# Two token blocks take turns while the first weights are decoded, with PSUM sums of their own

## The chip, the cores and the metric

The kernel runs on one core of one Trainium2 chip. The metric is the device time of one execution in microseconds (us); before the change the median of three runs is 1047.18 us. Five engines work in parallel, each through its own queue in order: TensorE (PE; its weight loads are PEld), VectorE (DVE), ScalarE (ACT), GpSimd (POOL) and SyncE (SP), which here only issues transfers. They wait for one another through semaphores.

## What is computed

A linear attention with a decaying state, then two feed-forward layers (cut from the reference):

```python
for t in range(S):                      # batch 4, 8 heads, S = 768, head_dim 48
    state = alpha[:, :, t, :, None] * state + einsum('bhd,bhe->bhde', k[:, :, t], v[:, :, t])
    y[:, :, t] = einsum('bhd,bhde->bhe', q[:, :, t], state)
x = y as (3072 tokens, 384)
h = x @ w_in                            # 384 -> 2048
x = (h * cos(h)) @ w_out                # 2048 -> 384
g = x @ w_gate                          # 384 -> 1536
out = (silu(g) * (x @ w_val)) @ w_out2  # 1536 -> 384
```

The weights arrive as 64-bit floats. The kernel decodes each into a pair of 32-bit parts (a rounded part and its remainder).

## The kernel before

**Blocks and slots.** The 3072 tokens are six blocks (0 to 5) of 512, each made of four chunks of attention (chunks 0 to 3 make block 0, 8 to 11 block 2, and so on). The first layer runs in 16 slots per block, one for every 128 columns of `w_in`. In a slot TensorE makes nine passes of 512 columns for the hidden values (`hidden`, tile `h`, two PSUM banks in turn). ScalarE and VectorE make h·cos(h) from them: add the magic constant (L455), subtract (L458), sine and square (L460, L461), product (L469). The product frees the bank of `h`. ScalarE rounds the result to `ghi` (L491) and GpSimd takes the remainder `glo` (L492). Three slots later (`LAG`) TensorE makes the nine passes of the contraction with `w_out` into three PSUM banks `y0` to `y2`, which add up over the 16 slots of the block and are then spilled (`spill`, L505). Slots are numbered here in the order in which they run, from 0.

**Units.** The 16 pairs (`w_in` and `w_out` of one slot) are units 0 to 15. One unit is fetched by SyncE into one of two buffers (`raw`, L117, 768 KB) and decoded by a generator, `decode`: absolute value and low bits on ScalarE (L75, L76), floor (L81), shift (L82) and sign (L86) on VectorE, an addition on GpSimd (L91, called the tail below), a cast on ScalarE (L156), and the remainder half on VectorE and half on GpSimd (L164). A buffer is free for the unit after next when the sign step has read it.

**Attention.** The eight chunks of blocks 0 and 1 run ahead of everything, three steps of the stream apart. The others are spread over the slots of the block before theirs. A chunk has: two scans with a reciprocal between them on VectorE (L255, L259, L262), two products on GpSimd (L256, L263), scores `sc` (L283), a transpose `tp` (L289), two masked copies on VectorE (L285, L295), a state update `up` (L299) and the output `o` (L309, L313) on TensorE. `sc`, `o` and `tp` have three PSUM banks of their own (`psa`). Chunks 6 and on are loaded into two buffers in turn (`qka_124` and `qka_125`), each free when the output of the chunk two before has been read.

**The order.** The program is written slot by slot; a scheduler that is no part of the file then sets the order on each engine. In block 0 each slot asks for the units up to its number plus two, and for three more steps of the decode (`steps`); nothing of block 1 runs before block 0 has had its 16 slots.

Of the kernel before, what the change touches and what calls it, by code (L numbers as in the profile page):

```python
# [26 lines left out]
C = 128  # L27
# [66 lines left out]
class Fast:  # L94
    def __init__(self, tc, qka0, qka, v, w, maskd, x2d, out):
        self.tc, self.nc = tc, tc.nc
        self.qka0, self.qka, self.v, self.maskd = qka0, qka, v, maskd
        self.w = w
        self.x2d, self.out = x2d, out
        self.pairs = {}  # L100
        self.raws = {}
        self.ready = 0
        self.anchor = None
        self.xt = {}
        self.x2t = {}
        self.vt = {}
        self.queue = []
        self.pending = []
        self.masked = {}


# [127 lines left out]
    def attn(self, ch):  # L239
# [32 lines left out]
        yield  # L272

        if not front:
            places = [(self.psa, "sc", 1), (self.psa, "o", 1)]
        elif ch % 2:
            places = [(self.ps, "y1", 1), (self.ps, "y2", 1)]
        else:
            places = [(self.ps, "h", 2)] * 2
# [6 lines left out]
        if not last:  # L286
            tp = self.psa.tile([128, PAIRS, C], F32, name="tp", tag="tp", bufs=1)
            for p in range(PAIRS):
# [7 lines left out]
        if not last:  # L296
            up = self.psa.tile([128, PAIRS, 2, D], F32, name="up", tag="sc" if front else "tp", bufs=1)
            for p in range(PAIRS):
# [6 lines left out]
        else:  # L305
            o = self.psa.tile([128, PAIRS, C], F32, name="o", tag="o", bufs=1)
        for p in range(PAIRS):
# [35 lines left out]
        yield  # L343


    def passes(self, key, acts, k, out, mk, start, stop):
# [24 lines left out]
    def run(self):  # L371
# [4 lines left out]
        for ch in range(NCH):  # L376
            i = self.slot_of(ch)
            p = last_in.get(i)
            when = max(0, begin[ch] - AHEAD) if p is None else begin[p] + (6 if p < B else 8)
            if ch >= NFRONT:  # L380
                when = max(when, quick)
# [39 lines left out]
    def phase1(self, stream):  # L421
# [8 lines left out]
        def steps(blk, f, j):  # L430
            if blk == 0:
                self.weights(dec, F1, 1)
            elif blk == NB - 1 and f >= 2 and j:
                self.weights(self.dec, W2, 1)
# [8 lines left out]

        slots = [(blk, f) for blk in range(NB) for f in range(F1)]
        nsteps = [PERIOD * B] * NB
        nsteps[FRONT] += STAGES - PERIOD
        for blk, f in slots:
            if blk == 0:
# [15 lines left out]
            if FRONT <= blk + 1 < NB:  # L464
                nticks = [spread(min(2 * f + j, 28), 28, nsteps[blk + 1]) if 2 * f + j < 28 else 0 for j in range(2)]
            for _ in range(nticks[0]):
# [19 lines left out]
    def later(self, name, blk, f, nf, s, finish):  # L486
# [10 lines left out]
        if len(self.queue) > LAG:  # L497
            key, g, blk, nf, finish = self.queue.pop(0)
            if key[1] == 0:
                self.acc = [self.ps.tile([128, N], F32, name=f"y{m}", tag=f"y{m}", bufs=1) for m in range(KM)]  # L500
            self.contract(key, g, self.acc, key[1], nf)
            if key[1] == nf - 1:
                finish(blk, self.acc)

# [35 lines left out]
    def phase2(self):  # L540
        nc = self.nc
        self.xt = self.x2t
        slots = [(blk, f) for blk in range(NB) for f in range(F2)]
        for blk, f in slots:
# [18 lines left out]
        for fn in self.pending:  # L563
            fn()
        ob = self.gp.tile([128, KM, N], F32, name="ob", tag="big", bufs=BIG)
        for m in range(KM):
            for key, g, *_ in self.queue:
                self.contract(key, g, self.acc, key[1], F2, (m,))
            nc.scalar.copy(ob[:, m, : N // 2], self.acc[m][:, : N // 2])
            nc.vector.tensor_copy(ob[:, m, N // 2 :], self.acc[m][:, N // 2 :])  # L570
            self.put(NB - 1, ob, m, nc.sync)
# [227 lines left out]
```

## Time and profile before

| | us |
|---|---|
| median of three runs (1046.47 to 1047.54) | 1047.18 |
| the profiled execution | 1045.69 |
| its span on the core | 1043.7 |
| TensorE busy in the span | 994.4 |
| VectorE, ScalarE, GpSimd busy | 542.7, 502.9, 432.3 |

The busy time of TensorE is no measure of its work, since passes overlap in the record: a pass of 512 columns is listed with some 0.4 us and starts 0.23 us after the one before. The stretches to look at are the decode of the first 16 units (up to about 155 us) and block 1 with block 2's chunks behind it (up to 253.5 us).

### The profile page before, as it was taken

What the parts mean: (1) busy time and instruction counts of PE and PEld (TensorE: products, weight loads), DVE (VectorE), ACT (ScalarE), POOL (GpSimd) and SP (SyncE); (2) the same over time, 40 slices, a digit from 0 to 9 for tenths busy, and PEclk for the clock granted to TensorE, in tenths of its full rate; (3) what the DMA queues carried; (4) which work ended last, traced back from release to release, by engine and by line L of the source; (5) the groups of instructions that cost most, each with busy time, mean ns of one, the idle gap of its engine ahead of it and who ended that gap; (6) DMA issues with size and microseconds to landing.
All of it is one profiled execution on the core that took longest, in us unless ns stands there. A gap on an engine that the chain in (4) does not pass through costs nothing.

```text
span 1043.7 us, 12822 instructions
## 1 busy us (share of the span) xinstructions
PE 994.4 (95%) x4902; PEld 814.2 (78%) x4902; DVE 542.7 (52%) x750; ACT 502.9 (48%) x912; POOL 432.3 (41%) x338
## 2 busy tenths in 40 slices
PE   7896778999999999999999899999999999999997
PEld 6784556888888888888887688888888888888886
DVE  6989996565556555555388997222222222222221
ACT  2567875665665666665687854221221211311211
POOL 4557885434343344333267675231232311321111
PEclk8899999999999999999999999999999999999999
DMA  9724350332332223142043351010110100100101
GB/s 269 181 70 143 127 146 1 92 66 42 72 72 54 72 43 60 38 101 91 1 137 106 121 181 62 10 52 1 31 31 1 31 30 1 31 1 1 31 1 33
DMA packets 26452, 68.63 MB, mean 66 GB/s; under 512 B 2160, under 2 KB 11504, under 8 KB 24432
## 3 DMA queue, kind: packets, MB, share of 16 engines
q1 hardware_dynamic: 16064, 59.09, 21.3%
q10 hardware_dynamic: 10320, 8.65, 2.5%
q8 instruction: 40, 0.66, 0.3%
q14 instruction: 28, 0.23, 0.1%
HBM read 58.30 MB, written 9.44 MB: 65 GB/s over the span
## 4 chain that ended last, share of the span: by engine, by line
PE 78%; DVE 11%; ACT 4%; POOL 1%; issue 1%; POOLq 0%; ACTq 0%
PE y L350 28%; PE h L350 28%; PE hx L350 14%; PE o L313 3%; DVE wa L86 3%; DVE wa L82 2%; PE sc L283 2%; PE o L309 2%; DVE wa L81 1%; DVE pair L164 1%; PE up L299 1%; DVE s L469 1%; DVE s L458 1%; ACT wa L75 1%; POOL glo L492 1%
## 5 line engine op out<-in xcount | busy, mean ns | idle before, releaser
L492 POOL TENSOR_TENSOR glo<-s,ghi 128x512 fp32r<-128x512 f32 x168 | 230.3, 1371 | 472.0 <-ACT ghi L491 434.8
L350 PE MATMUL y<-ghi,pair 128*128 128x512 f32 x936 | 320.4, 398 | 0.1
L350 PE MATMUL h<-xh,pair 128*128 128x512 f32 x882 | 304.7, 400 | 7.6 <-DVE s L469 7.6
L350 PEld LDWEIGHTS y<-ghi,pair 128*128 128x128 f32 x936 | 176.5, 189 | 40.1 <-ACT ghi L491 0.6
L350 PE MATMUL y<-glo,pair 128*128 128x512 f32 x468 | 185.4, 396 | 19.9 <-POOL glo L492 19.8
L350 PEld LDWEIGHTS h<-xh,pair 128*128 128x128 f32 x882 | 166.4, 189 | 48.1 <-DVE s L469 6.0
L491 ACT CAST ghi<-s 128x512 fp32r<-128x512 f32 x168 | 104.1, 619 | 167.3 <-DVE s L557 119.4
L554 DVE TENSOR_TENSOR s<-s,h 128x512 f32<-128x512 f32 x72 | 49.4, 686 | 249.3 <-ACT s L551 249.3
L350 PE MATMUL h<-xl,pair 128*128 128x512 f32 x441 | 172.9, 392 | 0.0
L350 PE MATMUL hx<-xh,pair 128*128 128x512 f32 x414 | 139.1, 390 | 0.0
L551 ACT ACTIVATE s<-h 128x512 f32<-128x512 f32 x72 | 43.0, 597 | 169.8 <-PE h L350 168.9
L350 PEld LDWEIGHTS y<-glo,pair 128*128 128x128 f32 x468 | 88.2, 188 | 45.5 <-POOL glo L492 27.6
L350 PEld LDWEIGHTS h<-xl,pair 128*128 128x128 f32 x441 | 83.4, 189 | 17.3
L469 DVE SCALAR_TENSOR_TENSOR s<-s,h 128x512 f32<-128x512 f32 x87 | 59.3, 682 | 68.5 <-ACT s L461 68.0
L458 DVE SCALAR_TENSOR_TENSOR s<-s,h 128x512 f32<-128x512 f32 x87 | 59.3, 681 | 64.7 <-ACT s L455 64.4
L350 PEld LDWEIGHTS hx<-xh,pair 128*128 128x128 f32 x414 | 77.7, 188 | 16.7
L91 POOL TENSOR_TENSOR wa<-wa,wk 128x768 int32<-128x768 int32 x34 | 70.6, 2076 | 38.9 <-DVE wa L86 38.9
L460 ACT ACTIVATE s<-s 128x512 f32<-128x512 f32 x96 | 60.3, 628 | 49.8 <-DVE s L458 49.8
L350 PE MATMUL hx<-xl,pair 128*128 128x512 f32 x207 | 80.6, 389 | 0.0
L455 ACT ACTIVATE s<-h,magic 128x512 f32<-128x512 f32 x87 | 59.7, 686 | 41.0 <-PE h L350 23.7
L557 DVE TENSOR_TENSOR s<-s,hx 128x512 f32<-128x512 f32 x72 | 49.4, 686 | 41.7 <-PE hx L350 41.3
L461 ACT ACTIVATE s<-s 128x512 f32<-128x512 f32 x96 | 60.5, 631 | 2.3
(107 smaller groups left out, 1212.4 us busy)
## 6 DMA issues: line engine op xcount, KB each, us to landing
raw<-w SPq DMA_DIRECT2D x34, 768.0 KB, 4.3
qka<-qka SPq DMA_DIRECT2D x36, 384.8 KB, 6.4
v<-vv SPq DMA_DIRECT2D x16, 288.0 KB, 6.5
x2d<-x ACTq DMA_DIRECT2D x6, 768.0 KB, 5.7
x2r<-x2d SPq DMA_DIRECT2D x6, 768.0 KB, 5.6
out<-ob ACTq DMA_DIRECT2D x15, 256.0 KB, 2.8
spare<-qka SPq DMA_DIRECT2D x4, 672.0 KB, 13.0
vpair<-vv SPq DMA_DIRECT2D x8, 288.0 KB, 12.9
```

The source lines that it names most:

```text
L91: nc.gpsimd.tensor_tensor(a, a, low, ALU.add)
L350: self.nc.tensor.matmul(out, lhsT=self.parts(key, wpart, mk), rhs=act, start=start and n == 0, stop=stop and n == 2,)
L455: ins = nc.scalar.activation(s, h, AF.Identity, bias=magic).ins
L458: nc.vector.scalar_tensor_tensor(s, s, MAGIC, h, ALU.subtract, ALU.subtract)
L460: nc.scalar.activation(s, s, AF.Sin, scale=HALF_TURN)
L461: nc.scalar.activation(s, s, AF.Square)
L469: nc.vector.scalar_tensor_tensor(s, s, 0.5, h, ALU.subtract, ALU.mult)
L491: nc.scalar.copy(hi, s)
L492: nc.gpsimd.tensor_sub(lo, s, hi.bitcast(F32))
L551: self.anchor = nc.scalar.activation(s, hg, AF.Sigmoid).ins
L554: nc.vector.tensor_tensor(s, s, hg, ALU.mult)
L557: nc.vector.tensor_tensor(s, s, hv, ALU.mult)
```

## The change

Block 0 and block 1 share the decode: two slots of block 0, then one of block 1, so that 24 slots are written where 16 were; block 1's last eight slots follow. In each of them two decode steps are asked for instead of three. Since both blocks now add up at once, block 1's sums take the three banks of the attention, and block 2's chunks, which run in block 1's last eight slots, take block 0's banks `y0` to `y2`, once they are spilled. Block 3's chunks are spread over half-slots 4 to 29 of block 2 instead of 0 to 27. The loads of chunks 8 and 9 are no longer held back to the end of the first part of the stream.

```diff
         if not front:
-            places = [(self.psa, "sc", 1), (self.psa, "o", 1)]
+            places = banks[0:2]
...
+    def banks(self, blk):
+        if blk == FRONT:
+            return [(self.ps, f"y{m}", 1) for m in range(KM)]
+        return [(self.psa, t, 1) for t in ("sc", "o", "tp")]
+
+    def sums(self, blk):
+        where = self.banks(0) if blk == 1 and self.joint else self.banks(FRONT)
+        return [pool.tile([128, N], F32, name=f"y{m}", tag=tag, bufs=bufs) for m, (pool, tag, bufs) in enumerate(where)]
...
-            if ch >= NFRONT:
+            if ch >= NFRONT + 2:
                 when = max(when, quick)
...
         def steps(blk, f, j):
-            if blk == 0:
-                self.weights(dec, F1, 1)
+            if blk < FRONT:
+                if j:
+                    self.weights(dec, F1, 1)
...
-        slots = [(blk, f) for blk in range(NB) for f in range(F1)]
+        slots = []
+        for f in range(F1):
+            slots.append((0, f))
+            if f % 2:
+                slots.append((1, f // 2))
+        slots += [(1, f) for f in range(F1 // 2, F1)]
+        slots += [(blk, f) for blk in range(2, NB) for f in range(F1)]
...
+        window = [(0, 0), (0, 0)] + [(0, 28)] * NB
+        window[FRONT] = (F1, 2 * F1 - 2)
+        window[FRONT + 1] = (4, 30)
...
             if key[1] == 0:
-                self.acc = [self.ps.tile([128, N], F32, name=f"y{m}", tag=f"y{m}", bufs=1) for m in range(KM)]
-            self.contract(key, g, self.acc, key[1], nf)
+                self.acc[blk] = self.sums(blk)
+            self.contract(key, g, self.acc[blk], key[1], nf)
```

What it does to the order on the engines, at the three places that matter below. Line numbers of the changed file are higher by 2 to 30.

VectorE behind the attention of chunk 7, before. The floor, shift and sign steps are L81, L82 and L86; `wa` is the unit under decode.

```order
L458 SCALAR_TENSOR_TENSOR s<-s,h 128x512
L334 TENSOR_TENSOR st_137<-st_137,up 48x4x48 x2
L81 TENSOR_SCALAR wa<-wa 128x768
L82 TENSOR_SCALAR wa<-wa 128x768
L340 SCALAR_TENSOR_TENSOR xl<-o,xh 96x3x128
L340 SCALAR_TENSOR_TENSOR xl<-o,xh 32x128 x3
L86 SCALAR_TENSOR_TENSOR wa<-raw,wa 128x768
```

The floor step here is that of unit 3, and it follows the state update of chunk 7 directly.

The same place now. L485 and L497 are the subtraction and the product of a slot, L257 and L264 the two scans of a chunk, `qka_124` is chunk 8 and `qka_125` chunk 9.

```order
L497 SCALAR_TENSOR_TENSOR s<-s,h 128x512
L485 SCALAR_TENSOR_TENSOR s<-s,h 128x512
L257 SCALAR_TENSOR_TENSOR qka_125<-qka_125,starts 112x516
L261 RECIPROCAL rb<-qka_125 112x32
L264 SCALAR_TENSOR_TENSOR qka_125<-qka_125,rb 112x512
L497 SCALAR_TENSOR_TENSOR s<-s,h 128x512
L485 SCALAR_TENSOR_TENSOR s<-s,h 128x512
L81 TENSOR_SCALAR wa<-wa 128x768
L82 TENSOR_SCALAR wa<-wa 128x768
L86 SCALAR_TENSOR_TENSOR wa<-raw,wa 128x768
```

Unit 3 now stands behind the scans of chunks 8 and 9 (those of chunk 8 are just ahead of these rows) and behind the products of slots 0, 1 and 2 and the subtractions of slots 1, 2 and 3.

SyncE at the start of the decode, before:

```order
L117 DMA raw<-w 128x768 x2
L236 DMA v<-vv 128x576
L117 DMA raw<-w 128x768 x14
L223 DMA qka_124<-qka 48x2052 x2
L223 DMA qka_125<-qka 48x2052 x2
```

and now:

```order
L119 DMA raw<-w 128x768 x2
L238 DMA v<-vv 128x576
L119 DMA raw<-w 128x768
L225 DMA qka_124<-qka 48x2052 x2
L225 DMA qka_125<-qka 48x2052 x2
L119 DMA raw<-w 128x768 x13
```

The loads of chunks 8 and 9 have moved from behind the fetch of unit 15 to ahead of that of unit 3.

VectorE in the middle of the decode, before (unit 12, with the remainder of unit 11 and the steps of two slots):

```order
L81 TENSOR_SCALAR wa<-wa 128x768
L82 TENSOR_SCALAR wa<-wa 128x768
L86 SCALAR_TENSOR_TENSOR wa<-raw,wa 128x768
L164 TENSOR_TENSOR pair<-wa,pair 128x384
L469 SCALAR_TENSOR_TENSOR s<-s,h 128x512
L458 SCALAR_TENSOR_TENSOR s<-s,h 128x512
```

and now (units 12 and 13, subtraction L485, product L497, remainder L166):

```order
L81 TENSOR_SCALAR wa<-wa 128x768
L82 TENSOR_SCALAR wa<-wa 128x768
L86 SCALAR_TENSOR_TENSOR wa<-raw,wa 128x768
L485 SCALAR_TENSOR_TENSOR s<-s,h 128x512
L166 TENSOR_TENSOR pair<-wa,pair 128x384
L81 TENSOR_SCALAR wa<-wa 128x768
L82 TENSOR_SCALAR wa<-wa 128x768
L485 SCALAR_TENSOR_TENSOR s<-s,h 128x512
L497 SCALAR_TENSOR_TENSOR s<-s,h 128x512
L86 SCALAR_TENSOR_TENSOR wa<-raw,wa 128x768
L497 SCALAR_TENSOR_TENSOR s<-s,h 128x512
L166 TENSOR_TENSOR pair<-wa,pair 128x384
```

Before, each unit goes with one slot. Now two units go with two slots, in pairs. Counted over the whole order, 13 products stand from the floor step of unit 3 to the remainder of unit 15, before and now; at that remainder 16 slots have had their product, where 13 had it before.

## Rows read from the trace of the kernel before

**Rows 1.** Windows: stretch, length, busy time of each engine (instructions), TensorE's granted clock, DMA share, GB/s.

```profile
94.00:153.50 59.50, 45.52 (x184) 32.88 (x184) 58.81 (x63) 46.09 (x69) 49.67 (x31) 1.00 0.47 146
...
175.00:253.50 78.50, 78.50 (x461) 66.10 (x461) 45.41 (x72) 48.47 (x98) 30.61 (x30) 1.00 0.31 66
```

**Rows 2.** Waits from 94 to 154 us: total, times, longest.

```profile
PE y L350 <- POOL glo L492: 13.2, 10, 1.4
```

**Rows 3.** Timeline, VectorE, one unit: start, length, engine, line, operation, out<-in.

```profile
106.34 0.67 DVE L458 SCALAR_TENSOR_TENSOR s<-s,h 128x512 f32<-128x512 f32 x1
106.94 1.02 DVE L81 TENSOR_SCALAR wa<-wa 128x768 f32<-128x768 f32 x1
107.99 1.27 DVE L82 TENSOR_SCALAR wa<-wa 128x768 int32<-128x768 int32 x1
109.29 1.90 DVE L86 SCALAR_TENSOR_TENSOR wa<-raw,wa 128x768 int32<-128x768 int32 x1
```

**Rows 4.** Timeline, GpSimd, the same unit and the start of the next.

```profile
105.52 2.02 POOL L91 TENSOR_TENSOR wa<-wa,wk 128x768 int32<-128x768 int32 x1 [0.99 <-DVE wa L86]
107.50 1.34 POOL L164 TENSOR_TENSOR pair<-wa,pair 128x384 fp32r<-128x384 f32 x1
108.79 1.59 POOL L492 TENSOR_TENSOR glo<-s,ghi 128x512 fp32r<-128x512 f32 x1
111.36 2.02 POOL L91 TENSOR_TENSOR wa<-wa,wk 128x768 int32<-128x768 int32 x1 [0.98 <-DVE wa L86]
```

**Rows 5.** Timeline, VectorE, a floor step of the first units.

```profile
66.64 1.41 DVE L81 TENSOR_SCALAR wa<-wa 128x768 f32<-128x768 f32 x1
```

**Rows 6.** Timeline, GpSimd, beside it.

```profile
66.63 1.00 POOL L164 TENSOR_TENSOR pair<-wa,pair 128x384 fp32r<-128x384 f32 x1 [1.23 <-ACT pair L156]
```

**Rows 7.** Timeline, VectorE, unit 3's floor step, unit 15's remainder, scans of chunks 8 and 9.

```profile
77.40 1.07 DVE L81 TENSOR_SCALAR wa<-wa 128x768 f32<-128x768 f32 x1
...
155.18 0.56 DVE L164 TENSOR_TENSOR pair<-wa,pair 128x384 fp32r<-128x384 f32 x1 [1.41 <-ACT pair L156]
155.66 2.03 DVE L255 TENSOR_TENSOR_SCAN qka<-qka,starts 112x516 f32<-112x516 f32 x1
...
158.12 1.72 DVE L262 TENSOR_TENSOR_SCAN qka<-qka,rb 112x512 f32<-112x512 f32 x1
...
165.43 2.33 DVE L255 TENSOR_TENSOR_SCAN qka<-qka,starts 112x516 f32<-112x516 f32 x1
...
168.19 1.92 DVE L262 TENSOR_TENSOR_SCAN qka<-qka,rb 112x512 f32<-112x512 f32 x1
```

**Rows 8.** Timeline, ScalarE, the cast of unit 2.

```profile
79.16 0.82 ACT L156 CAST pair<-wa 128x768 fp32r<-128x768 f32 x1
```

**Rows 9.** Timeline, TensorE: chunk 7's last output; hidden passes of slots 2, 18, 31 and 32.

```profile
75.96 0.60 PE L313 MATMUL o<-sm,vpair 128*96 128x128 f32 x4
...
83.25 0.48 PE L350 MATMUL h<-xh,pair 128*128 128x512 f32 x1 [4.63 <-DVE s L469]
...
83.95 1.05 PE L350 MATMUL h<-xh,pair 128*128 128x512 f32 x2
84.80 0.63 PE L350 MATMUL h<-xl,pair 128*128 128x512 f32 x1
...
175.07 1.16 PE L283 MATMUL sc<-qka 48*128 48x128 f32 x16
176.16 0.50 PE L350 MATMUL h<-xh,pair 128*128 128x512 f32 x1
...
249.40 0.40 PE L350 MATMUL h<-xh,pair 128*128 128x512 f32 x1
...
253.55 0.40 PE L350 MATMUL h<-xh,pair 128*128 128x512 f32 x1
```

**Rows 10.** Page, DMA issues: tile, queue, count, KB each, median us to landing.

```profile
raw<-w SPq DMA_DIRECT2D x34, 768.0 KB, 4.3
qka<-qka SPq DMA_DIRECT2D x36, 384.8 KB, 6.4
```

More of the change, by code (lines that the diff above doesn't have):

```diff
@@ L109, in __init__ @@
         self.masked = {}
+        self.acc = {}
+        self.joint = True
     def fetch(self, i):
@@ L272, in attn @@
         yield
+        banks = self.banks(blk)
         if not front:
-            places = [(self.psa, "sc", 1), (self.psa, "o", 1)]
+            places = banks[0:2]
         elif ch % 2:
@@ L286, in attn @@
         if not last:
-            tp = self.psa.tile([128, PAIRS, C], F32, name="tp", tag="tp", bufs=1)
+            pool, tag, bufs = banks[2]
+            tp = pool.tile([128, PAIRS, C], F32, name="tp", tag=tag, bufs=bufs)
             for p in range(PAIRS):
@@ L296, in attn @@
         if not last:
-            up = self.psa.tile([128, PAIRS, 2, D], F32, name="up", tag="sc" if front else "tp", bufs=1)
+            pool, tag, bufs = banks[0 if front else 2]
+            up = pool.tile([128, PAIRS, 2, D], F32, name="up", tag=tag, bufs=bufs)
             for p in range(PAIRS):
@@ L305, in attn @@
         else:
-            o = self.psa.tile([128, PAIRS, C], F32, name="o", tag="o", bufs=1)
+            pool, tag, bufs = banks[1]
+            o = pool.tile([128, PAIRS, C], F32, name="o", tag=tag, bufs=bufs)
         for p in range(PAIRS):
@@ L464, in phase1 @@
             if FRONT <= blk + 1 < NB:
-                nticks = [spread(min(2 * f + j, 28), 28, nsteps[blk + 1]) if 2 * f + j < 28 else 0 for j in range(2)]
+                lo, hi = window[blk + 1]
+                nticks = [spread(i - lo, hi - lo, nsteps[blk + 1]) if lo <= i < hi else 0 for i in (2 * f, 2 * f + 1)]
             for _ in range(nticks[0]):
@@ L499, in later @@
             if key[1] == 0:
-                self.acc = [self.ps.tile([128, N], F32, name=f"y{m}", tag=f"y{m}", bufs=1) for m in range(KM)]
-            self.contract(key, g, self.acc, key[1], nf)
+                self.acc[blk] = self.sums(blk)
+            self.contract(key, g, self.acc[blk], key[1], nf)
             if key[1] == nf - 1:
-                finish(blk, self.acc)
+                finish(blk, self.acc[blk])
     def spill(self, blk, y):
@@ L542, in phase2 @@
         self.xt = self.x2t
+        self.joint = False
         slots = [(blk, f) for blk in range(NB) for f in range(F2)]
@@ L565, in phase2 @@
         ob = self.gp.tile([128, KM, N], F32, name="ob", tag="big", bufs=BIG)
+        acc = self.acc[NB - 1]
         for m in range(KM):
             for key, g, *_ in self.queue:
-                self.contract(key, g, self.acc, key[1], F2, (m,))
-            nc.scalar.copy(ob[:, m, : N // 2], self.acc[m][:, : N // 2])
-            nc.vector.tensor_copy(ob[:, m, N // 2 :], self.acc[m][:, N // 2 :])
+                self.contract(key, g, acc, key[1], F2, (m,))
+            nc.scalar.copy(ob[:, m, : N // 2], acc[m][:, : N // 2])
+            nc.vector.tensor_copy(ob[:, m, N // 2 :], acc[m][:, N // 2 :])
             self.put(NB - 1, ob, m, nc.sync)
```

## The prediction

> **What bounds the kernel now.** I read the windows by stage first. From 175 us to the end of block 1 TensorE is busy for 78.50 of 78.50 us [rows 1]: there only TensorE's own work counts, and what other engines do is free. From 94 to 153.5, while units are decoded, VectorE is busy for 58.81 of 59.50 and TensorE for 45.52 [rows 1], and TensorE's largest wait is for GpSimd's `glo`, ten times up to 1.4 us [rows 2]. So the decode sets the pace there, and TensorE has room. That room is what the change is about.
>
> How the decode spends a unit stands in the timelines of the two engines side by side. A unit takes 111.36 - 105.52 = 5.84 us [rows 4] and goes with one slot. VectorE's floor step (106.94, 1.02 long) ends 0.42 behind the end of GpSimd's tail; GpSimd's remainder ends 0.88 behind that floor step; the shift 0.42 behind the remainder; `glo` 1.12 behind the shift; the sign 0.81 behind `glo`; and the next tail begins 0.17 later [rows 3, 4]. 2.02 + 0.42 + 0.88 + 0.42 + 1.12 + 0.81 + 0.17 = 5.84: the two engines take turns, none of these steps overlaps one of the other engine's. What does overlap is VectorE's remainder, product and subtraction, which fit under the 2.02 of the tail [rows 3, 4]. The same is seen at 66.64, where a floor step needs 1.41 because GpSimd is at work until 67.63 [rows 5, 6], again 0.42 behind it.
>
> The Trainium skill has the rule for this (SBUF — State Buffer, section "SBUF: two separate sides"): VectorE in its faster modes and GpSimd share a port pair by an exclusive lock for a whole instruction. The rows agree. By it an added slot costs the decode its `glo`, 1.12; by VectorE's busy time alone it would cost product and subtraction, some 1.2 by their pitch. Over 13 units and 13 slots the two come out alike; they differ over the pairs below.
>
> **The change part by part.** *What the order does.* The slots are written three to two units, but that is not how they stand: two units go with two slots in the middle of the decode, and from unit 3's floor step to unit 15's remainder there are 13 products, as before. So block 1 does not fill TensorE's room in the decode. What is gained is three slots ahead of unit 3, which run while VectorE waits, and these are what the sum turns on.
>
> *Ahead of unit 3.* Its floor step began at 77.40 [rows 7]. Now, from the cast of unit 2, which ends at 79.98 [rows 8], VectorE has: the remainder of unit 2 (to 80.5), a subtraction (0.6), chunk 8's scans, a product and a subtraction (1.2), chunk 9's scans, a product and a subtraction (1.2). The first scan pair took from 155.66 to 159.8, 4.1 us; the second from 165.43 to 170.0, 4.6 (both from the first scan's start to the next step's) [rows 7]. 80.5 + 0.6 + 4.1 + 1.2 + 4.6 + 1.2 = 92.2, some 15 us later than before. With every scan as short as the shortest there (1.72) it would be 91. The fetch hides behind this: chunk 9's load is issued when chunk 7's last output is done, at 76.6 [rows 9], and lands 6.4 later; unit 3's fetch is queued behind it on SyncE, and if it starts to flow only then, it lands 4.3 later [rows 10], at 87.4. Were both half as long again, chunk 9 would land at 86.2, about when its scan's turn comes, and unit 3 at 92.6, which would cost 1 to 3 us: that is the upper end here, with unit 4 to 15's fetches queued behind.
>
> *Units 3 to 15.* 13 units with 13 slots at 5.84 make 75.9. To this comes what the tail no longer covers: in the pairs one subtraction and one product stand between shift and sign, 1.2 per two units in the clean case, partly beside a `glo`. I count 4.2 such us over the order and take 3, with 0 and 5.5 as ends. By VectorE's busy time alone this term would be 0. So unit 15's remainder is at 92.2 + 75.9 + 3 = 171.1, where it was at 155.18 [rows 7].
>
> *A place to compare.* Ahead of the hidden passes of slot 18, TensorE has the same work in both orders (18 sets of hidden passes, 135 passes of contraction), apart from chunk 8's scores. Before, it starts them at 176.16, and at 175.07 without the scores [rows 9]. Now the product of slot 16, which frees the bank, follows unit 15's remainder; with its sine, square and the waits that is 1.4 later, 172.5. Lead: 2.6 us. From there to slot 32 (253.55 [rows 9]) TensorE was never idle [rows 1], so the lead stays if the second half of block 1 stays full.
>
> *Block 2's chunks in the last eight slots.* Their work is the same; it now falls into slots 26 to 31. Chunk 8's scores and transpose wait for the spill of `y0`, `y1` and `y2`: ScalarE and VectorE reach it some 0.3 and 0.2 us late. Chunk 10 can be loaded only when chunk 8's output is read, and with 6.4 [rows 10] its scans start some 2 us after VectorE is free; what reaches TensorE by way of the bank that `o` and the second `sc` share is about 0.5. Together I take 1.1, with 0.3 (the spill alone) and 4 (a stall like that for each chunk) as ends. Chunk 12 has to wait for block 1's spill in the same way: 0.6, from 0 to 1.5.
>
> *The rest.* The sums in other banks cost nothing in themselves, since the passes are the same. Half-slots 4 to 29 for block 3's chunks leave one slot in hand, under a busy TensorE. From block 3 on the order is the same.
>
> Sum: -2.6 + 1.1 + 0.6 = -0.9. It is made against the profiled execution of 1045.69 (span 1043.7), 1.5 below the median; I put the same difference on the median: 1046.3.
>
> **The rivals.** *The slots fill the room,* as the change says: eight slots of 4.15 each (253.55 - 249.40 [rows 9]), 33.2 us of TensorE, would go into the decode for 8 x 1.12 of `glo`, 9 us, and the time would be near 1047.2 - 24 = 1023. Against it is the order: the slots of block 1 don't stand there.
>
> *The chain runs tighter.* If unit 3 starts at 91 and the tails cover both products of a pair, unit 15 is done at 91 + 75.9 = 166.9 and slot 18 starts at 168.3: a lead of 6.8, less 1.7, gives -5.1, 1042.1. For it: both terms have that as their lower end. It decides from 169.7 for unit 15's remainder on, which gives the 2.1 us of 0.2%.
>
> *The pairs leave VectorE uncovered,* the slower one. If every unit has a subtraction and a product that no tail covers, 13 x 1.2 = 15.6 replace the 3: +12.6, 1058.9. For it: VectorE has nothing to spare (58.81 of 59.50 [rows 1]), and a subtraction now waits for ScalarE, which has the casts of two units between. It decides from 6.0 us for this term, 0.46 per unit, where the total is +2.1; its middle is 1052.5.
>
> *The clock.* Behind 4.63 us of idling, slot 2's passes ran 0.43 us apart (two of them from 83.95 to 84.80), where 18 passes in 4.15 make 0.23 [rows 9]. If the pairs made TensorE idle long enough each time, 36 passes of two slots would take 15.5 us instead of 8.3, more than the 11.7 of two units, and add 3.8 per pair: +23, 1070. Against it: over the ten waits of up to 1.4 us the granted clock stayed at 1.00 [rows 1, 2], and the pairs leave gaps of 1 to 2 us. The Trainium skill names it as a failure of its own (TensorE: Matmul & The Clock Gate, section "HAM oscillation — how this bites in real kernels"): bursts with waits between them that each start at the lower clock. By that rule this rival is live; the rows speak against it.
>
> **How the numbers follow.** Within 0.2%, which is 2.1 us and about what a measurement of this kernel can tell from no change: 0.45, with 1046.3 as the likeliest and 1044.5 to 1049.2 as its own range. Tighter chain 0.30 and filled room 0.03: faster 0.33. Uncovered pairs 0.20, clock 0.02: slower 0.22. The range is 1040.0 to 1053.0: it holds the first case, all but the end of the tighter chain (0.05 left out) and more than half of the uncovered pairs (0.08 left out); with the filled room and the clock 0.18 is outside.
>
> **What would show it.** Unit 3's floor step at 91 to 94 with both chunks' scans ahead of it; unit 15's remainder near 171; slot 18's hidden passes near 172.5; TensorE idle for about 1 us from slot 25 to 32, and slot 32 near 252. The prediction is wrong if unit 3's floor step waits for its fetch, if unit 15's remainder lies outside 167 to 176, if the granted clock falls below 0.9 between 115 and 170, or if slots 26 to 31 show more than 4 us of idle time on TensorE.

## The result, and the profile after

The changed kernel takes 1058.44 us (median of four runs, 1056.30 to 1060.02) where the kernel before, in its runs beside it, takes 1047.36: a ratio of 1.0105, 95% interval 1.0085 to 1.0124, so it is slower by some 11 us. The prediction was 1046.3 with a range of 1040 to 1053; sign and range are both wrong. The profiled execution took 1058.35, its span is 1056.6.

The windows of the changed kernel, columns as in [rows 1]: the first two stretches are those shown there, the third is the start of block 2.

```profile
94.00:153.50 59.50, 45.35 (x169) 34.31 (x170) 55.63 (x57) 42.38 (x63) 42.90 (x28) 0.91 0.35 120
175.00:253.50 78.50, 77.98 (x439) 64.29 (x438) 43.08 (x64) 46.67 (x91) 31.55 (x28) 1.00 0.24 52
262.00:282.00 20.00, 17.05 (x75) 13.22 (x74) 10.03 (x13) 9.44 (x17) 7.56 (x6) 0.91 0.11 42
```

In the decode TensorE does no more than before (169 instructions where there were 184), at a granted clock of 0.91 on average instead of 1.00. In block 1 it is still full. New is the third row: 3 us of idle time and a lower clock at a place that was full. The same stretch in the kernel before:

```profile
262.00:282.00 20.00, 20.00 (x118) 16.80 (x117) 11.71 (x19) 12.98 (x27) 8.11 (x8) 1.00 0.41 94
```

Where the time is lost is read from the starts of the slots' hidden passes. TensorE's timeline of the changed kernel, slots 18, 32 and 47, and of the kernel before, slot 47 (for 18 and 32 see [rows 9]):

```profile
177.08 0.50 PE L367 MATMUL h<-xh,pair 128*128 128x512 f32 x1
...
259.01 0.40 PE L367 MATMUL h<-xh,pair 128*128 128x512 f32 x1
...
347.93 0.39 PE L367 MATMUL h<-xh,pair 128*128 128x512 f32 x1
```

```profile
336.22 0.40 PE L350 MATMUL h<-xh,pair 128*128 128x512 f32 x1
```

Slot 18 is 177.08 - 176.16 = 0.92 late, and 2.0 with chunk 8's scores, which are still to come (175.07 in [rows 9]). Slot 32 is 259.01 - 253.55 = 5.46 late, when block 2's chunks are done in both. Slot 47 is 347.93 - 336.22 = 11.7 late, and that stays so to the end of the first layer. So 2.0 are lost in the decode, 3.4 from slot 18 to 32, 6.2 from 32 to 47. The last 1.4 come early in the second layer, after a wait of some 2.4 us that both kernels have. Together these are 13.0; the spans of the two profiled executions are 12.9 apart, the medians 11. The windows there, of the kernel before and of the changed one:

```profile
586.00:606.00 20.00, 17.64 (x77) 14.06 (x76) 19.01 (x21) 14.23 (x21) 11.75 (x7) 1.00 0.37 130
```

```profile
598.00:618.00 20.00, 17.65 (x70) 13.91 (x70) 19.01 (x22) 14.48 (x21) 11.47 (x8) 0.91 0.40 133
```

The idle time is the same; the granted clock was 0.91 here and 1.00 before. Nothing is changed at that place, and the profiles of the kernels below show it either way; what decides it stays open.

*The decode.* VectorE's timeline of the changed kernel (answers to [rows 3] and [rows 7]): unit 3's floor step, the sign step of one unit in the middle and what follows up to that of the next, unit 15's remainder.

```profile
91.80 2.79 DVE L81 TENSOR_SCALAR wa<-wa 128x768 f32<-128x768 f32 x1
...
137.78 0.96 DVE L86 SCALAR_TENSOR_TENSOR wa<-raw,wa 128x768 int32<-128x768 int32 x1
138.65 0.68 DVE L497 SCALAR_TENSOR_TENSOR s<-s,h 128x512 f32<-128x512 f32 x1
139.25 1.91 DVE L166 TENSOR_TENSOR pair<-wa,pair 128x384 fp32r<-128x384 f32 x1
141.08 0.68 DVE L485 SCALAR_TENSOR_TENSOR s<-s,h 128x512 f32<-128x512 f32 x1
141.68 0.78 DVE L81 TENSOR_SCALAR wa<-wa 128x768 f32<-128x768 f32 x1
142.50 1.54 DVE L82 TENSOR_SCALAR wa<-wa 128x768 int32<-128x768 int32 x1
144.07 0.96 DVE L86 SCALAR_TENSOR_TENSOR wa<-raw,wa 128x768 int32<-128x768 int32 x1
...
174.90 0.78 DVE L166 TENSOR_TENSOR pair<-wa,pair 128x384 fp32r<-128x384 f32 x1
```

GpSimd beside the middle ones (answers to [rows 4]):

```profile
138.91 1.84 POOL L91 TENSOR_TENSOR wa<-wa,wk 128x768 int32<-128x768 int32 x1 [1.58 <-DVE wa L86]
140.70 1.35 POOL L166 TENSOR_TENSOR pair<-wa,pair 128x384 fp32r<-128x384 f32 x1
142.00 1.62 POOL L520 TENSOR_TENSOR glo<-s,ghi 128x512 fp32r<-128x512 f32 x1
145.18 1.83 POOL L91 TENSOR_TENSOR wa<-wa,wk 128x768 int32<-128x768 int32 x1 [1.55 <-DVE wa L86]
```

The remainder on VectorE (L166) took 0.55 in the kernel before (0.56 in [rows 7]). Here it takes 1.91: it starts behind the tail (138.91) and ends at 141.16, 0.41 behind the tail's end at 140.75. In 11 of the 13 units from unit 3 on it takes 1.28 to 1.91: GpSimd is at work already when it is issued, in eight of the 11 a product or a subtraction now stands between the sign step and it. In the unit shown, each step behind it then ends behind a later instruction of GpSimd than before: the floor step (142.46) 0.41 behind GpSimd's remainder (142.05), the shift (144.04) 0.42 behind `glo` (143.62). The sign step, which ran beside `glo` in [rows 3, 4], comes after it, and GpSimd idles for 1.55 where it idled for 0.98. The units are not alike (from one tail's start to the next it is 4.3 to 8.0), so this one shows the mechanism and not the average. From unit 3's floor step to unit 15's remainder it is 174.90 - 91.80 = 83.1.

*Block 2's chunks.* TensorE, the scores (`sc`) of chunks 8 and 9:

```profile
210.21 1.99 PE L286 MATMUL sc<-qka 48*128 48x128 f32 x16 [0.16 <-ACT x L536]
...
218.75 1.16 PE L286 MATMUL sc<-qka 48*128 48x128 f32 x8
...
221.79 1.13 PE L286 MATMUL sc<-qka 48*128 48x128 f32 x8
```

Before, all 16 take 1.16 at one go [rows 9]. Here chunk 8's are stretched to 1.99, and chunk 9's come in two pieces of about 1.15 each. Counted from each start to the next, the scores of the four chunks take 6.70 instead of 4.36, so 2.3 of the 3.4.

*Block 3's first chunk.* TensorE at the start of block 2, L536 being the spill:

```profile
268.74 0.50 PE L367 MATMUL h<-xh,pair 128*128 128x512 f32 x1 [1.15 <-DVE s L497]
...
274.47 1.16 PE L286 MATMUL sc<-qka 48*128 48x128 f32 x8 [1.79 <-ACT x L536]
...
275.98 1.16 PE L286 MATMUL sc<-qka 48*128 48x128 f32 x8
...
277.41 0.56 PE L367 MATMUL h<-xh,pair 128*128 128x512 f32 x1
277.77 0.63 PE L367 MATMUL h<-xl,pair 128*128 128x512 f32 x1
278.20 1.05 PE L367 MATMUL h<-xh,pair 128*128 128x512 f32 x2
```

Chunk 12's scores wait 1.79 for block 1's spill, come in two pieces too, and behind that the passes start 0.43 apart instead of 0.23, at the lower of the two clock levels. The wait of 1.15 is for a product that stands behind chunk 12's scans on VectorE:

```profile
266.17 1.93 DVE L264 TENSOR_TENSOR_SCAN qka<-qka,rb 112x512 f32<-112x512 f32 x1
268.02 0.66 DVE L497 SCALAR_TENSOR_TENSOR s<-s,h 128x512 f32<-128x512 f32 x1
```

### The profile page after: what moved, and what is told of

Same layout as the page of the kernel before. It is cut to its first block, busy times and chain, and to the rows that moved or that the text cites. A ratio compares the mean times of both kernels' runs of the same rounds, so it can differ in the third digit from the quotient of the medians.

```text
span 1056.6 us, 12835 instructions
## 1 busy us (share of the span) xinstructions
PE 1004.9 (95%) x4902; PEld 822.8 (78%) x4902; DVE 549.5 (52%) x750; ACT 503.1 (48%) x912; POOL 432.5 (41%) x338
## 4 chain that ended last, share of the span: by engine, by line
PE 70%; DVE 13%; ACT 7%; issue 2%; POOL 2%; POOLq 0%; ACTq 0%
PE y L367 25%; PE h L367 24%; PE hx L367 14%; PE o L319 3%; DVE pair L166 2%; PE sc L286 2%; DVE s L485 2%; DVE s L497 2%; DVE wa L82 2%; DVE wa L81 2%; DVE wa L86 2%; PE o L315 1%; ACT s L487 1%; ACT s L482 1%; ACT s L488 1%
## 5 line engine op out<-in xcount | busy, mean ns | idle before, releaser
L367 PE MATMUL h<-xh,pair 128*128 128x512 f32 x882 | 308.3, 404 | 24.0 <-DVE s L497 19.5
L367 PEld LDWEIGHTS h<-xh,pair 128*128 128x128 f32 x882 | 169.0, 192 | 67.5 <-DVE s L497 24.7
L367 PE MATMUL h<-xl,pair 128*128 128x512 f32 x441 | 175.3, 398 | 0.0
L497 DVE SCALAR_TENSOR_TENSOR s<-s,h 128x512 f32<-128x512 f32 x87 | 59.4, 683 | 68.5 <-ACT s L488 68.1
L485 DVE SCALAR_TENSOR_TENSOR s<-s,h 128x512 f32<-128x512 f32 x87 | 59.3, 681 | 65.6 <-ACT s L482 65.3
```

Source lines behind the costliest of these rows:

```text
L367: self.nc.tensor.matmul(out, lhsT=self.parts(key, wpart, mk), rhs=act, start=start and n == 0, stop=stop and n == 2,)
L485: nc.vector.scalar_tensor_tensor(s, s, MAGIC, h, ALU.subtract, ALU.subtract)
L497: nc.vector.scalar_tensor_tensor(s, s, 0.5, h, ALU.subtract, ALU.mult)
```

## The experiments

All were timed beside the kernel before, and ratios are to it. The table has, read from each trace, how late a slot starts against the kernel before, each counted from its own slot 0 (which starts at 67.6 to 72.4). At slot 23 only the kernel before and before768 have done chunks 8 and 9 (each 1.09 for scores, 0.32, 0.72 and 2.55 for the rest, 4.68 together); for the other kernels 9.4 is added there to make the work alike. inturn_wide has done part of them at that slot and has no entry.

| kernel | ratio (95% interval) | slot 23 | slot 32 | slot 47 |
|---|---|---|---|---|
| changed | 1.0105 (1.0085 to 1.0124) | 1.6 | 5.7 | 11.9 |
| inturn | 1.0083 (1.0065 to 1.0102) | 0.5 | 2.9 | 9.1 |
| hold | 1.0130 (1.0113 to 1.0147) | 0.3 | 6.7 | 14.5 |
| late12 | 1.0052 (1.0035 to 1.0069) | 1.9 | 5.9 | 7.5 |
| anch_hold | 1.0055 (1.0037 to 1.0072) | -5.7 | 0.9 | 8.6 |
| inturn_wide | 0.9999 (0.9988 to 1.0010) | | 0.2 | 0.1 |
| share768 | 1.0073 (1.0051 to 1.0094) | -1.1 | 2.5 | 7.2 |
| anch12 | 1.0014 (1.0003 to 1.0026) | -5.7 | 0.9 | 2.5 |
| anch12_one | 1.0014 (0.9996 to 1.0032) | -5.7 | 3.5 | 4.8 |
| three | 1.0189 (1.0169 to 1.0209) | 9.3 | 12.9 | 20.8 |
| third12 | 0.9993 (0.9981 to 1.0005) | -4.0 | 1.1 | 1.0 |
| quarter12 | 0.9972 (0.9961 to 0.9983) | -2.3 | -1.1 | -1.1 |
| quarter768 | 0.9939 (0.9920 to 0.9958) | -6.5 | -5.2 | -5.3 |
| before768 | 0.9946 (0.9926 to 0.9967) | -4.4 | -4.4 | -4.4 |
| quarter_free | 0.9970 (0.9957 to 0.9983) | -2.4 | -1.1 | -1.2 |

**inturn** undoes the change in the decode alone.

```diff
-        for f in range(F1):
-            slots.append((0, f))
-            if f % 2:
-                slots.append((1, f // 2))
...
+        slots = [(blk, f) for blk in range(NB) for f in range(F1)]
...
-            if blk < FRONT:
-                if j:
-                    self.weights(dec, F1, 1)
+            if blk == 0:
+                self.weights(dec, F1, 1)
...
-            if ch >= NFRONT + 2:
+            if ch >= NFRONT:
```

> The slots of blocks 0 and 1 stand one after the other again, with three decode steps in each slot of block 0 and the loads of chunks 8 and 9 held back; only the new banks, block 2's chunks in block 1's last eight slots and block 3's chunks in half-slots 4 to 29 stay. Theory A, by the place where the slots of the changed kernel fall behind those of before: 2.0 us in the decode, 3.4 in slots 26 to 31, 6.2 from slot 32 to 47. Then this order keeps 9.6 of it: 1047.4 + 9.6 = 1057.0, slot 18 at 175, slot 32 some 3.4 and slot 47 some 9.6 behind that of before. Theory B, the prediction's: the two edits behind the decode cost 1.1 + 0.6, and the rest hangs on the decode: 1049.1.

1054.47 us. Of the 11 us, 7.9 stay with the decode as it was. Theory B falls; theory A's time was 2.5 too high. From slot 32 to 47 it loses 9.1 - 2.9 = 6.2, exactly as the changed kernel does, with the same two waits (1.18 and 1.76); up to slot 32 it loses less than I had read for that stretch.

**hold** changes the last of these three places alone.

```diff
-            if ch >= NFRONT + 2:
+            if ch >= NFRONT:
```

> Only the loads of chunks 8 and 9 are held back as before; two slots of block 0 and one of block 1 still take turns. The scans leave the place ahead of unit 3, and the order pairs the units less. Theory A: the decode is earlier by the 8.7 us of the scans (unit 3's floor step at about 82, unit 15's remainder at about 160), but TensorE gains nothing of it, since the three slots that ran beside the scans now run in the decode as well: slot 18 at 175 to 176.5, the time 1056.5 to 1058. Theory B: the scans ahead of unit 3 are plain delay: slot 18 at 168.4, the time 1049.7.

1060.42: worse by 2. Unit 15's remainder comes at 165.29, 9.6 earlier than in the changed kernel (not at theory A's 160), and slot 18 at 175.60, as theory A has it: TensorE gains nothing, since no slot runs ahead of unit 3 any more and 15 products instead of 13 stand inside the decode. Theory B falls. Theory A's time was still too low, as chunk 8's scores now wait 1.02 for the spill of block 0. The scores there, and the window around them:

```profile
209.70 1.99 PE L286 MATMUL sc<-qka 48*128 48x128 f32 x16 [1.02 <-ACT x L536]
```

```profile
205.00:215.00 10.00, 8.98 (x42) 7.04 (x42) 4.62 (x7) 5.59 (x10) 3.53 (x3) 0.84 0.03 12
```

The clock falls behind that wait (0.84), which it did not behind the 0.16 of the changed kernel.

**late12** moves block 3's chunks by four half-slots.

```diff
-        window[FRONT + 1] = (4, 30)
+        window[FRONT + 1] = (8, 30)
```

> The changed kernel with block 3's chunks in half-slots 8 to 29 instead of 4 to 29, so that chunk 12's scores come when block 1's sums are spilled. Theory A: the two waits of 1.15 and 1.79 us, the scores in two pieces (1.07 more) and the low clock behind them (some 1.9) go: 1058.4 - 5 = 1053.4, slot 47 some 6.7 behind that of before. Theory B: the wait only moves, since the same four chunks have less room: 1058.4, within 1.

1051.74, 6.7 less than the changed kernel, somewhat more than theory A's 5. TensorE at the same place:

```profile
267.92 0.50 PE L367 MATMUL h<-xh,pair 128*128 128x512 f32 x1 [1.15 <-DVE s L497]
...
278.57 1.16 PE L286 MATMUL sc<-qka 48*128 48x128 f32 x16
```

The wait for the spill is gone and the scores are in one piece. Over the same 20 us as above the clock is whole:

```profile
262.00:282.00 20.00, 18.85 (x93) 14.71 (x92) 11.35 (x16) 12.94 (x23) 7.61 (x6) 1.00 0.11 41
```

The wait of 1.15 for a product stayed, and no low clock followed it; from slot 32 to 47 only 1.6 are lost instead of 6.2. So 4.6 hung on the wait for the spill, far more than its own 1.79. The rest of the 6.7 lies outside this stretch and is not placed.

**anch_hold** makes the order do what it says: each decode step of blocks 0 and 1 is issued behind the first step of a slot, and three slots really stand to two units.

```diff
-            if blk == NB - 1:
+            if blk < FRONT or blk == NB - 1:
                 self.anchor = ins
...
-            if ch >= NFRONT + 2:
+            if ch >= NFRONT:
```

> As hold, and each decode step is tied to the first step of the slot ahead of it, so that three slots really stand to two units (counted over the order: three products per two units). Theory A, the decode has room for it on TensorE: two units take 2 x 5.84 + 1.12 for the third remainder of a slot = 12.8 to 14.5, unit 15's remainder at 82 + 6.5 x that = 165 to 176, with 19 to 20 slots through by then where 13 were; TensorE is 10 to 15 ahead of the changed kernel from there on: 1043 to 1048. Theory B, VectorE and GpSimd take turns so closely that each added slot costs what it gives, 4.1 us: 1056 to 1058.

1052.29, above theory A's range (1043 to 1048). Two units now take 126.62 - 111.67 = 14.95. VectorE's floor steps:

```profile
111.67 0.96 DVE L81 TENSOR_SCALAR wa<-wa 128x768 f32<-128x768 f32 x1 [0.61 <-ACT wa L75]
...
117.16 0.78 DVE L81 TENSOR_SCALAR wa<-wa 128x768 f32<-128x768 f32 x1
...
126.62 0.56 DVE L81 TENSOR_SCALAR wa<-wa 128x768 f32<-128x768 f32 x1
```

14.95 - 2 x 5.84 = 3.3 for the added slot, which is worth 4.15 to TensorE. The lead at slot 23 is 5.7, and it is lost again by slot 32: block 2's chunks have six slots, a hidden pass waits 1.7 for its product and the first scores 1.23 for the spill, and from 202 to 212 us the granted clock is 0.83.

**inturn_wide** is inturn with the chunks given room; the changed banks stay.

```diff
-        window[FRONT] = (F1, 2 * F1 - 2)
-        window[FRONT + 1] = (4, 30)
+        window[FRONT] = (8, 30)
+        window[FRONT + 1] = (8, 30)
```

> As inturn (the slots one after the other), with block 2's chunks over half-slots 8 to 29 of block 1 instead of its last eight slots, and block 3's over 8 to 29 too; the banks stay the changed ones. Theory A: the loss behind the decode comes from the chunks standing close together and from the two waits for a spill, not from the banks as such: it is gone, 1047 within 1. Theory B: the other banks cost by themselves (scores that wait for two banks of different age): 2 to 4 us stay, 1049 to 1051.

1046.0, ratio 0.9999: all 7.9 of inturn are gone. Theory A holds: the banks cost nothing, the places of the chunks cost all of it.

**share768** gives the whole remainder to VectorE.

```diff
-SHARE = 384
+SHARE = 768
```

> The changed kernel with the whole remainder of units 0 to 15 on VectorE, none on GpSimd; the order of the decode steps and slots behind unit 3 stays word for word. Theory A, the two engines take turns: each unit is spared GpSimd's 1.34 and pays some 0.45 on VectorE, of which the sum of a unit shows 0.88 - 0.45 = 0.4: units 3 to 15 take 83.1 - 13 x 0.4 = 77.5, the time is 1052.8; with both engines' whole difference 83.1 - 13 x 0.9 = 71.4, 1046.7. Theory B, VectorE's own steps and what they wait for are the limit: +13 x 0.45 = 5.9, 1064.

1053.82, 4.6 less than the changed kernel. From unit 3's floor step to unit 15's remainder it is 171.83 - 91.53 = 80.3, so 2.8 less, about half of what theory A's first figure had (13 x 0.4 = 5.2, which gives 77.9 and not its 77.5); slot 18 is 3.1 earlier. The rest is behind the decode, where the two waits at chunk 12 stayed (1.2 and 1.8) and no low clock followed them, as the window of 255 to 285 us of share768 shows:

```profile
255.00:285.00 30.00, 27.08 (x142) 21.86 (x141) 15.33 (x24) 17.61 (x33) 10.45 (x11) 1.00 0.18 47
```

From slot 32 to 47 it loses 7.2 - 2.5 = 4.7, where the changed kernel loses 6.2: so the low clock there is worth some 1.6. Theory B (+5.9) falls: VectorE has more work and the decode is shorter.

**anch12** is anch_hold with late12's window.

> anch_hold and late12 together: the three slots to two units, and block 3's chunks in half-slots 8 to 29. Theory A: the two parts add: 1052.3 - 6.7 = 1045.6. Theory B: what anch_hold gains in the decode is lost again at block 2's chunks, which wait for the spill of block 0 and let the clock fall, whatever comes later: the gain of late12 alone shows and the lead at slot 32 stays near 7 us over that of the changed kernel; the time is 1045 to 1047, the same as before, but TensorE shows the low clock near slot 26.

1047.68: theory B. The lead of 5.7 at slot 23 is again lost by slot 32, with the same waits and the low clock (0.83 from 202 to 212 us).

**anch12_one** moves block 2's chunks by one half-slot more.

```diff
-        window[FRONT] = (F1, 2 * F1 - 2)
+        window[FRONT] = (F1 + 1, 2 * F1 - 1)
```

> As anch12, with block 2's chunks one half-slot later (half-slots 17 to 30 of block 1). Theory A: chunk 8's scores come after block 0's spill, so the wait of 1.23 us, the slow scores (0.83 more) and the low clock behind it (some 1.5) go, and chunk 11's output is still in time: 1045.6 - 3.5 = 1042. Theory B: what is won at chunk 8 is lost at the end of the block, where the hidden passes of block 2 wait for chunk 11: 1045.6 or up to 3 more.

1047.89, where theory B has it, but the edit did not do what either theory starts from: chunk 8's scores still wait for the spill. TensorE at chunk 8's scores and at the first slot of block 2:

```profile
203.28 2.11 PE L286 MATMUL sc<-qka 48*128 48x128 f32 x16 [1.28 <-ACT x L536]
...
257.56 0.50 PE L367 MATMUL h<-xl,pair 128*128 128x512 f32 x1 [0.97 <-DVE xl L346]
```

So nothing is won at chunk 8 (the granted clock is 0.83 there as in anch12), and the first hidden passes of block 2 now wait for chunk 11's output. Whether scores that come behind the spill would gain in six slots is not shown.

**three** asks for three decode steps in each slot.

```diff
             if blk < FRONT:
-                if j:
-                    self.weights(dec, F1, 1)
+                self.weights(dec, F1, 1)
```

> The changed kernel with three decode steps asked for in each slot of blocks 0 and 1 instead of two. The slots still take turns, unit 3 still stands behind the scans of chunks 8 and 9, and 13 units still go with 13 slots, but the last four units stand one to a slot as in the kernel before (floor, shift, sign, remainder, product, subtraction), the others in pairs. Theory A: what a unit costs hangs on that order, since a remainder that stands behind a product on VectorE has to wait for GpSimd's tail: the last four units take 5.84 each with a remainder of 0.55, those in pairs 6.4 with remainders of 1.3 to 1.9; unit 15's remainder is 2 to 3 earlier, the time 1055.5 to 1056.5. Theory B: the second block costs by itself, in whatever order (its sums, its remainders on GpSimd): 6.4 for the last four units too, 1058.4.

1067.07, slower than everything, though the decode ends earlier: unit 15's remainder is at 169.97, 4.9 before that of the changed kernel. My count of slots was wrong: 13 products stand ahead of it, where the changed kernel has 16. Three slots more behind the decode, at 4.15, are 12.5, less the 4.9: 7.6 of the 8.6 measured. So the end of the decode is not what counts, but the slots that TensorE has done by then. On the order within a unit theory A holds. VectorE, a unit among the pairs and two of the regular ones:

```profile
137.43 1.83 DVE L166 TENSOR_TENSOR pair<-wa,pair 128x384 fp32r<-128x384 f32 x1
...
150.94 1.02 DVE L81 TENSOR_SCALAR wa<-wa 128x768 f32<-128x768 f32 x1
...
155.13 0.55 DVE L166 TENSOR_TENSOR pair<-wa,pair 128x384 fp32r<-128x384 f32 x1
...
156.80 1.01 DVE L81 TENSOR_SCALAR wa<-wa 128x768 f32<-128x768 f32 x1
```

Where the remainder stands right behind the sign step it takes 0.55 and a unit 156.80 - 150.94 = 5.86 with one product, with the two blocks still taking turns. The eight units from unit 3 on, mostly in pairs, take 5.98 each (92.71 to 140.56), with only five products among them.

**third12 and quarter12** are anch12 with three or four slots of block 0 to one of block 1, which leaves eight or nine slots for block 2's chunks (quarter12 shown).

```diff
-            if f % 2:
-                slots.append((1, f // 2))
-        slots += [(1, f) for f in range(F1 // 2, F1)]
+            if f % 4 == 3:
+                slots.append((1, f // 4))
+        slots += [(1, f) for f in range(4, F1)]
...
-        window[FRONT] = (F1, 2 * F1 - 2)
+        window[FRONT] = (12, 30)
```

> As anch12, with three slots of block 0 to one of block 1 (five instead of eight slots of block 1 in the decode) and block 2's chunks in half-slots 14 to 29 of block 1, behind the earlier spill of block 0. Theory A: each added slot gains about 1.06 (8.5 us of lead at slot 25 for eight in anch12), so 5.3 here; the chunks have eight slots instead of six and lose 2 to 3 instead of 6.7: 1047 - 5.3 + 2.5 = 1044. Theory B: the loss at the chunks does not hang on the room but on the wait for the spill, and stays at 6.7: 1048.4.

> As third12 with four slots of block 0 to one of block 1 (four of block 1 in the decode) and block 2's chunks in half-slots 12 to 29. Theory A: 4 x 1.06 = 4.2 gained in the decode, 1 to 2 lost at the chunks, which have nine slots: 1047 - 4.2 + 1.5 = 1044.3. Theory B: 1047 - 4.2 + 6.7 = 1049.5.

third12 is no faster than before (0.9993), between the two theories. quarter12 is (0.9972, some 3 us), near theory A's time but with other sizes: 2.3 is gained at slot 23 instead of 4.2, and 1.2 of it is lost by slot 47.

**quarter768 and before768** set `SHARE` to 768 in quarter12 and in the kernel before.

> quarter12 with the whole remainder of units 0 to 15 on VectorE, as share768 did it for the changed kernel (4.6 us faster there). Theory A: the turns of VectorE and GpSimd are what the decode costs in every order, so a like amount is gained: 1044.7 - 4 = 1040.5. Theory B: with a slot less in the decode GpSimd is no longer short, and VectorE, which gets 0.45 more per unit, is: 1044.7, up to 3 more.

> The kernel before with one number changed: the whole remainder of units 0 to 15 on VectorE. Nothing takes turns between blocks here. Theory A: what quarter768 gained over quarter12 is a cost of the two engines' turns in any order: each unit is spared 0.88 - 0.45 = 0.4, unit 15's remainder comes 5 to 6 earlier, TensorE's slots with it: 1042. Theory B: in the regular order the remainder stands ahead of the tail and is 0.55 long, so the tail starts 0.45 later for each unit and GpSimd's shorter turn only makes up for it: 1047 within 1.5; then the gain needs the interleaved order.

1040.61 both, 0.9939 and 0.9946: theory A's time in both. One number in the kernel before gives 0.5%, and two blocks that take turns add nothing that can be told from it. VectorE and GpSimd in before768, for [rows 3] and [rows 4]:

```profile
109.33 0.96 DVE L86 SCALAR_TENSOR_TENSOR wa<-raw,wa 128x768 int32<-128x768 int32 x1
110.21 0.95 DVE L164 TENSOR_TENSOR pair<-wa,pair 128x768 fp32r<-128x768 f32 x1
...
112.27 0.99 DVE L81 TENSOR_SCALAR wa<-wa 128x768 f32<-128x768 f32 x1
```

```profile
110.46 2.39 POOL L91 TENSOR_TENSOR wa<-wa,wk 128x768 int32<-128x768 int32 x1 [1.58 <-DVE wa L86]
112.81 1.61 POOL L492 TENSOR_TENSOR glo<-s,ghi 128x512 fp32r<-128x512 f32 x1
116.00 2.40 POOL L91 TENSOR_TENSOR wa<-wa,wk 128x768 int32<-128x768 int32 x1 [1.58 <-DVE wa L86]
```

The half of the remainder that VectorE takes over costs it 0.95 - 0.55 = 0.4, GpSimd loses 1.34, and a unit takes 116.00 - 110.46 = 5.54 instead of 5.84. The tail pays for the remainder ahead of it: it is listed with 2.39 here, 2.02 in [rows 4], and 1.84 at 138.91 in the changed kernel, where a product is ahead.

The 4.4 by which slot 23 is early are not 13 times this 0.30, though. The first units take longer here, unit 15's remainder is only 2.6 earlier (152.56), not theory A's 5 to 6, and slot 14 is 1.8 early. Another 2.5 come at slot 15: there the kernel before waits for the `glo` that stands behind GpSimd's last remainders. TensorE and GpSimd before:

```profile
158.80 0.79 PE L350 MATMUL y<-glo,pair 128*128 128x512 f32 x1 [2.59 <-POOL glo L492]
```

```profile
154.23 2.37 POOL L164 TENSOR_TENSOR pair<-wa,pair 128x384 fp32r<-128x384 f32 x2
156.56 2.19 POOL L492 TENSOR_TENSOR glo<-s,ghi 128x512 fp32r<-128x512 f32 x1
```

**quarter_free** is quarter12 without the tie.

```diff
-            if blk < FRONT or blk == NB - 1:
+            if blk == NB - 1:
                 self.anchor = ins
```

> quarter12 without the tie of the decode steps to the slots: the scheduler may draw them ahead. Counted over the order, 13 or 14 products stand ahead of unit 15's remainder instead of 15. Theory A: the slots that then stand behind the decode cost TensorE their time again: 1046 to 1048. Theory B: the tie does nothing: 1044.7.

1044.32, as quarter12. It doesn't answer what it was made for: in the trace as many products stand ahead of unit 15's remainder as in quarter12 (16), so the number did not change. It shows that with few added slots the scheduler's own order is as good.

## Why the prediction was wrong, point by point

*What bounds the kernel.* Right: TensorE sets the end from block 1 on, and the turns of VectorE and GpSimd set the decode. before768 is the best evidence: with less work for GpSimd and more for VectorE the stretch from unit 3's floor step to unit 15's remainder goes from 77.8 to 152.56 - 78.28 = 74.3, and TensorE's slots come 4.4 earlier.

*Ahead of unit 3.* Right in what stands there, in part lucky in the number: its floor step began at 91.80 (92.2 predicted), behind both chunks' scans, and did not wait for its fetch. Chunk 8's scans began at 81.86 instead of 81.1, and chunk 9's took 90.62 - 87.17 = 3.4 instead of 4.6; the two misses cancel. The floor step took 2.79, since GpSimd was busy.

*Units 3 to 15: the first step that failed.* 78.9 predicted, 83.1 measured; unit 15's remainder at 174.90 instead of 171.1, slot 18 at 177.08 instead of 172.5. The lead of 2.6 was a lag of 2.0. Two terms were too small. The base: 13 units at 5.84 make 75.9, but the kernel before itself takes 155.18 - 77.40 = 77.8 for this stretch [rows 7], since unit 15's remainder stands 7.33 behind its floor step and not 5.84; 1.9 were missing before anything changed. And what the tail no longer covers: I took the 1.2 of two steps per pair as the price and 3 as the sum; it was 83.1 - 77.8 = 5.3, which is 0.4 per unit, just inside the upper end of 5.5.

What was wrong in the reading: I said that the remainder on VectorE fits under the tail. In [rows 4] the tail begins at 105.52; the remainder began before it, at 105.27, right behind the sign step, and was out of the way. Put behind a product, it is blocked until the tail ends, and each step behind it ends behind a later instruction of GpSimd. The Trainium skill has this too (SBUF — State Buffer, section "Who interferes with whom"): a VectorE instruction with two inputs in SBUF contends with a GpSimd instruction that reads SBUF, and the one that issues second is blocked; the remainder has two such inputs, product and subtraction read `h` from PSUM. The rows agree (0.55 ahead of the tail, 1.91 behind it). I had drawn on that page without asking which steps its rule covers.

That the order of the steps within a unit is the cause is shown inside three, where both kinds of unit stand in one run with both blocks at work. That it is the blocked remainder, and not the other steps of a pair, is read from the rows and not shown apart: no run moves the remainder alone, and how the 5.3 divide was not measured. share768 shows only that GpSimd's share of the work counts.

*Block 2's chunks.* 1.1 predicted with 4 as the upper end, 3.4 measured. The mechanism was partly right, a late spill, but the sizes that I had were idle times, and TensorE shows hardly any (0.16). Most of the cost, 2.3, is in how the scores run: stretched to 1.99 for chunk 8, and in two pieces for chunk 9, 1.08 and 1.05 from start to next start instead of 1.09 for both. That this is because the banks come free one by one fits the wait for the spill at chunk 8, but no run shows it apart; the other 1.1 was not placed.

*Block 3's chunk 12: the step that failed most.* 0.6 predicted with 1.5 as the upper end, 6.2 measured from slot 32 to 47, and inturn has the same 6.2 with the decode of before. I had priced the wait for the spill and nothing that hangs on it. The wait was 1.79; with it came the scores in two pieces (1.08 more) and the low clock, with passes 0.43 apart (1.6 by share768). 1.79 + 1.08 + 1.6 = 4.5, and late12, which takes the wait for the spill away and leaves the rest, gets 4.6 back. Of the 1.6 that stay in late12, 1.15 is the wait for the product behind chunk 12's scans, which the prediction does not have. I had asked of the clock only in the decode.

*From block 3 on* I had no difference. Early in the second layer the profiled execution loses 1.4 to the clock; some profiles of the other kernels do and some do not, so it is no effect of the change that these runs show. The misses add up to 4.6 in the decode, 2.3 and 5.6 at the chunks and this 1.4, 13.9, where the two profiled executions miss the forecast of -0.9 by 1058.35 - 1045.69 + 0.9 = 13.6.

*The rivals.* The uncovered pairs came nearest in the time, with 1058.9, but by luck: that rival wants 15.6 where the order cost 5.3, less than the 6.0 from which it decides. The time is 1058.4 because the edits behind the decode cost 7.9 (inturn) and the decode about 3 (at slot 47 the changed kernel is 11.9 late and inturn 9.1; the medians are 4.0 apart). The clock in the decode did not decide: it was 0.91 over the 59.5 us of the first window and 0.95 from 115 to 170 us, not the lower level in every pair. That the slots do not fill the room was right, and anch_hold shows what it would have brought: 3.3 us of decode for 4.15 us of TensorE.

*What I said would prove it wrong* did not: unit 3's floor step did not wait for its fetch, unit 15's remainder lies inside 167 to 176, and slots 26 to 31 show 0.5 us of idle time on TensorE and still lose 3.4. The granted clock, 0.95 from 115 to 170 us, fell below 0.9 only in parts of it (0.80 from 155 to 160). Idle time was the wrong measure for a cost that lies in slower work, and I had no sign for chunk 12, where most was lost.

Two small sums of the prediction are off and change nothing: unit 3's fetch would land at 76.6 + 6.4 + 4.3 = 87.3, not 87.4, and the tighter chain decides from 171.1 - 1.2 = 169.9, not 169.7.

## What to carry to other kernels

Before moving work behind a spill or into fewer slots, ask what the first instruction behind the wait will cost, not only how long the wait is: here 1.8 us of waiting became 4.6. For engines that block one another, list which steps block, and look at which of them issues first. And when the pace is set by two engines taking turns, a smaller share for the slower one (one constant, -0.5%) can be worth more than filling the room it leaves.

## What the runs showed of the hardware

Eight scores of one half of the array's rows take as long as 16 that alternate between the halves: 1.16 for eight (274.47 above) and 1.16 for sixteen (278.57 in late12). The Trainium skill says of tiles of the array (TensorEngine Tiling (Array Packing), section "Key Properties") that they operate independently and can run in parallel; the rows agree, and show that it is lost when the two halves are issued apart.

Whether the clock falls behind a wait is not told by the wait alone: a wait of 1.15 was followed by a whole clock in late12, 1.15 and 1.79 one after the other by 0.91 over 20 us in the changed kernel, while share768, with the wait for the same spill, shows no low clock there; and a wait of some 2.4 us early in the second layer was followed by either level in different profiles.

Half a remainder (128 x 384) costs GpSimd 1.34 [rows 4] and VectorE 0.4 on top of its own half, where it stands ahead of the tail (before768).
